# Slot pairs in four two-bank PSUM tiles, 1024-wide operations and one plan of step times, for a linear-attention and gMLP kernel

## Chip, cores, metric

One core of a Trainium2 chip. The time is the device time of one execution in microseconds (us). Five engines work side by side, each in the order of its own queue: TensorE (PE in the profile; its weight loads are PEld), VectorE (DVE), ScalarE (ACT), GpSimd (POOL) and SyncE (SP), which only issues DMAs here. PSUM is the memory that TensorE writes its results to; these kernels use it as eight banks, each for a tile of 128 x 512 fp32 values.

## The reference, cut to what matters

```python
# attention, for batch 8, heads 8, sequence 576, head width 64, 128 features
def phi(x):
    proj = x @ w_phi
    proj = proj - max(abs(proj), last axis)
    return concat([exp(proj), exp(-proj)])
q_p, k_p = phi(q), phi(k)
kv  = sum_s k_p v ;  z = sum_s k_p
x   = (q_p kv) / (q_p z + 1e-6)              # heads side by side: [8, 576, 512]
# gMLP block
h   = gelu_tanh(x @ w_in) ; u, v = halves of h
v_n = layernorm(v) * g_ln
v_s = w_sg @ v_n + b_sg                      # over the sequence
out = x + (u * v_s) @ w_out
```

## The kernel before: the parts that matter

The work is cut into eight halves k = 0 to 7 (two batches and four heads each) and four blocks u = 0 to 3 of gMLP. A half has nine slots of 128 rows. For each half: q and k are loaded (`qks`), merged into one tile (`qk`, VectorE), transposed (`qkT`, by DMA, for half 0 by TensorE), projected and exponentiated (`nat`, tiles `psk`, `psq`, `kp`), summed against the scaled values (`kvsum`, tile `pkv`; GpSimd scales the values), and turned into the attention output (`projnum`, tiles `pp`, `qp`, `pn`, `pxt`). Two halves feed one gMLP block: `win_v`, `norm`, `win_u`, `gate`, `wout`.

```python
psN = ctx.enter_context(tc.tile_pool(name="psN", bufs=4, space=PSUM))   # eight single banks
psA = ctx.enter_context(tc.tile_pool(name="psA", bufs=2, space=PSUM))   # in three pools
psM = ctx.enter_context(tc.tile_pool(name="psM", bufs=2, space=PSUM))

def load_qk(k, res, behind=None):
    qks = stage.tile([128, 2, HH, NS, D], FP16, tag="qks", name="qks")  # one buffer
    for t, src in enumerate((q, k_)):
        for ins in load(nc.gpsimd, ...):
            if behind is not None:                                      # held back behind the
                tc.add_manual_dep(ins.ins, behind.ins.name, sync, ...)  # transposes of a half
            yield
...
# nat, one slot: two banks, 512-wide operations
psk = psN.tile([128, HH, 128], F32, ...); psq = psN.tile([128, HH, 128], F32, ...)
... 4 + 4 matmuls ...
nc.vector.tensor_reduce(out=MK[:, n, :], in_=psk[:], axis=AX.X, op=ALU.max, ...)
nc.vector.tensor_reduce(out=MQ[:, n, :], in_=psq[:], axis=AX.X, op=ALU.max, ...)
for e in range(2):
    nc.scalar.activation(out=kp[:, e], in_=psk[:], func=AF.Exp, scale=(1.0, -1.0)[e])
...
# the main loop: the merge of half k+2 comes first, its load was issued during the stage before
qT[k + 2], last = prep(qks.pop(k + 2))
w.append((load_qk(k + 3, qks, last), 9, LD0, LD1))
weave(...)                       # interleaves the streams of one stage
...
# the last block
weave((win_v(res, range(NS)), 10, 0, 1))
weave((norm(res, 0, 5, (0, 1)), 7, 0, 0.5), (win_u(res, [(0, 288), (288, 288)]), 9, 0, 1))
weave((gate(res, 0), 9, 0, 1), (norm(res, 5, 9, ()), 6, 0, 0.5))
weave((win_u(res, [(576, 288), (864, 288)]), 9, 0, 1))
weave((wout(res, range(0, 4)), 5, 0, 1)); weave((gate(res, 1), 9, 0, 1)); weave((wout(res, range(4, 9)), 6, 0, 1))
```

## Time and profile before

| | before |
|---|---|
| time, median | 389.38 us (388.74 to 389.77, 3 runs) |
| span of the profiled execution | 381.7 us (this one execution took 383.46 us, a fast one) |
| busy: TensorE, VectorE, ScalarE, GpSimd | 291.3, 265.0, 246.3, 137.0 us |
| DMA: bytes moved, mean rate over the span | 40.04 MB, 105 GB/s |

The lines of the profile that matter are in the prediction. A row of the table of stretches is: start and end, length, then busy us and instruction count of PE, PEld, DVE, ACT, POOL, then the granted TensorE clock, the DMA share (mean busy share of 16 DMA engines; a little over 1 is possible as it is computed from packet times) and GB/s. A row of the timeline is: start, length, engine, line, operation, out<-in, shape, count, and in brackets how long the engine had been idle and what ended that. A row of the waits is: who waited <- for whom, then us in total, times, longest.

### The profile page before, as it was taken

How to read it: one execution, taken by the hardware profiler on the slowest of the kernel's cores; microseconds unless marked ns; L12 is line 12 of the kernel's file. 1: busy time of each engine (PE TensorE's matmuls, PEld its weight loads, DVE VectorE, ACT ScalarE, POOL GpSimd, SP SyncE). 2: the span in 40 equal slices, each digit the busy share in tenths (PEclk: the TensorE clock that was granted, in tenths of full speed). 3: DMA queues.
4: the chain of work that ended last, by engine and by line, in shares of the span. 5: the costliest groups of instructions: out<-in, count | busy, mean ns of one | idle time of the engine just before them, and what ended most of it. 6: DMA issues, size and time to landing. Idle time of an engine off the chain costs nothing.

```text
span 381.7 us, 7907 instructions
## 1 busy us (share of the span) xinstructions
PE 291.3 (76%) x3037; PEld 199.5 (52%) x3037; DVE 265.0 (69%) x680; ACT 246.3 (65%) x525; POOL 137.0 (36%) x173
## 2 busy tenths in 40 slices
PE   0263633847879989987896987977998898987894
PEld 0153522536645666754464765755566675644562
DVE  5499426876689998768569885675799944479230
ACT  1165314955986898569777892597779945672422
POOL 7247650592880229208800196046000830000000
PEclk9998585886589998999999899989999998799999
DMA  7996997288599705591992059902500020210024
GB/s 134 164 221 100 174 203 125 48 97 177 102 127 199 95 2 64 141 233 34 167 272 49 3 64 223 199 2 85 180 3 2 0 114 2 84 56 0 2 111 139
DMA packets 65094, 40.04 MB, mean 105 GB/s; under 512 B 36256, under 2 KB 61728, under 8 KB 65056
## 3 DMA queue, kind: packets, MB, share of 16 engines
q1 hardware_dynamic: 46128, 27.65, 29.3%
q0 software_dynamic: 18928, 11.88, 23.4%
q8 instruction: 24, 0.39, 0.4%
q14 instruction: 14, 0.11, 0.1%
HBM read 33.55 MB, written 9.44 MB: 113 GB/s over the span
## 4 chain that ended last, share of the span: by engine, by line
PE 29%; ACT 20%; DMA 14%; DVE 13%; POOL 12%; issue 9%; SPq 1%; ACTq 0%; DVEq 0%; POOLq 0%
DMA qks<-in_k_dram 8%; ACT qp L329 7%; ACT kp L258 7%; PE pu L399 5%; POOL qks L77 5%; POOL vx L274 5%; PE pw L439 4%; PE pv L383 4%; PE po L456 3%; PE pkv L313 2%; PE pn L348 2%; DVE bst L388 2%; DMA qkT<-qk 2%; DVE MK L252 2%; DMA wn<-in_moe_w_sg_dram 2%
## 5 line engine op out<-in xcount | busy, mean ns | idle before, releaser
L274 POOL TENSOR_TENSOR vx<-vs,vx 128x1024 f16<-128x1024 f32 (+2 forms) x48 | 72.1, 1520 | 104.0 <-ACT vx L265 100.0
L258 ACT ACTIVATE kp<-psk 128x512 f16<-128x512 f32 x144 | 81.7, 653 | 34.6 <-DVE MK L252 30.0
L329 ACT ACTIVATE qp<-pp 128x512 f16<-128x512 f32 x128 | 73.6, 685 | 15.8 <-PE pp L324 15.8
L252 DVE TENSOR_REDUCE MK<-psk 128x4 f32<-128x512 f32 x72 | 49.1, 681 | 8.6 <-PE psk L249 7.9
L254 DVE TENSOR_REDUCE MQ<-psq 128x4 f32<-128x512 f32 x72 | 49.0, 680 | 1.2 <-PE psq L251 1.2
L439 PE MATMUL pw<-WsgT,vt 128*128 128x288 f16 x256 | 45.8, 293 | 5.3 <-DVE uT L443 5.1
L249 PE MATMUL psk<-wk,qkT 128*128 128x128 f16 x288 | 33.8, 241 | 15.4 <-ACT qkT L232 9.6
L251 PE MATMUL psq<-wq,qkT 128*128 128x128 f16 x288 | 32.5, 242 | 15.2 <-DVE MQ L254 11.9
L443 DVE TENSOR_TENSOR uT<-pw,uT 128x288 f16<-128x288 f32 x64 | 28.6, 450 | 18.3 <-PE pw L441 16.5
L348 PEld LDWEIGHTS <-qp 128*128 128x128 f16 x512 | 23.8, 105 | 31.2 <-ACT qp L329 26.3
L348 PE MATMUL pn<-kvz,qp 128*128 128x65 f16 x512 | 29.5, 205 | 13.8 <-ACT qp L329 11.5
L401 ACT ACTIVATE uT<-pu 128x384 f16<-128x384 f32 (+1 forms) x52 | 24.3, 466 | 19.2 <-PE pu L399 18.4
L103 DVE COPY qk<-qks 128x2304 f16<-128x2304 f16 x16 | 14.6, 918 | 31.6 <-DMA qks<-in_k_dram 16.3
L460 ACT ACTIVATE osb<-po 128x512 f32<-128x512 f32 x36 | 24.2, 681 | 18.6 <-PE po L456 14.2
L399 PE MATMUL pu<-xT,Win 128*128 128x384 f16 (+1 forms) x208 | 35.6, 312 | 0.3 <-ACT vt L386 0.2
L383 PE MATMUL pv<-Win,xT 128*128 128x512 f16 x144 | 34.0, 384 | 1.2 <-ACT vt L386 1.1
L249 PEld LDWEIGHTS <-qkT 128*128 128x128 f16 x288 | 22.9, 108 | 22.6 <-ACT qkT L232 11.2
L439 PEld LDWEIGHTS <-vt 128*128 128x128 f16 x256 | 24.5, 99 | 18.6 <-issue 10.4
L251 PEld LDWEIGHTS <-qkT 128*128 128x128 f16 x288 | 23.5, 110 | 18.7 <-issue 17.4
L313 PE MATMUL pkv<-vx,kp 128*128 128x65 f16 x512 | 28.8, 208 | 5.0 <-POOL vx L274 5.0
L324 PE MATMUL pp<-qkT,wqm 66*128 66x512 f16 x72 | 29.8, 427 | 3.4 <-ACT kp L258 3.1
L456 PE MATMUL po<-Wout,uT 128*128 128x512 f16 x108 | 31.5, 386 | 0.0
(93 smaller groups left out, 520.6 us busy)
## 6 DMA issues: line engine op xcount, KB each, us to landing
out_dram<-osb SPq DMA_DIRECT2D x32, 256.0 KB
vs<-in_v_dram SPq DMA_DIRECT2D x16, 320.0 KB
vs<-in_v_dram SPq DMA_DIRECT2D x16, 256.0 KB
qks<-in_q_dram POOLq DMA_DIRECT2D x16, 160.0 KB, 4.0
qks<-in_k_dram POOLq DMA_DIRECT2D x16, 160.0 KB, 6.1
qks<-in_q_dram POOLq DMA_DIRECT2D x16, 128.0 KB, 4.7
qks<-in_k_dram POOLq DMA_DIRECT2D x16, 128.0 KB, 6.1
Win<-in_moe_w_in_dram POOLq DMA_DIRECT2D x1, 1024.0 KB, 10.8
```

The source lines that it names most:

```text
L249: nc.tensor.matmul(psk[:, i, :], qkT[:, n, i, :], wk[:], start=True, stop=True)
L251: nc.tensor.matmul(psq[:, i, :], qkT[:, n, i, :], wq[:], start=True, stop=True)
L252: nc.vector.tensor_reduce(out=MK[:, n, :], in_=psk[:], axis=AX.X, op=ALU.max, apply_absolute_value=True)
L254: nc.vector.tensor_reduce(out=MQ[:, n, :], in_=psq[:], axis=AX.X, op=ALU.max, apply_absolute_value=True)
L258: nc.scalar.activation(out=kp[:, e], in_=psk[:], func=AF.Exp, scale=(1.0, -1.0)[e])
L274: nc.gpsimd.tensor_tensor(out=vx[e][:, :, x0:x0 + nn, 0:64], in0=vs[:, :, n0:n1, :], in1=vx[e][:, :, x0:x0 + nn, 64:65].broadcast_to([128, ...
L329: nc.scalar.activation(out=qp[:, e], in_=pp[:], func=AF.Exp, scale=(1.0, -1.0)[e])
L348: nc.tensor.matmul(pn[:, i, :], lhs, rhs, start=(x == 0), stop=(x == len(terms) - 1))
L383: nc.tensor.matmul(pv[:], xT[:, c, n * 128:n * 128 + 128], Win[:, c, DF2:DFF], start=(c == 0), stop=(c == 3))
L399: nc.tensor.matmul(pu[:, 0:w], Win[:, c, d * 128:d * 128 + 128], xT[:, c, t0:t0 + w], start=(c == 0), stop=(c == 3))
L439: nc.tensor.matmul(pw[:], vts[5 * i + m][:, dd], WsgT[:, m, c0:c0 + 288], start=(m == 0), stop=False)
L456: nc.tensor.matmul(po[:], uT[:, d, cs], Wout[:, d, :], start=False, stop=(d == 3))
```

## The change

Its intent: fewer and wider instructions (slots 0-1, 2-3, 4, 5-6, 7-8 handled as groups), all PSUM in one pool of four two-bank tiles that every stage shares, loads ahead of time, and one list of step times for the whole kernel in place of stage-wise weaving. A step may demand that others have been emitted first. Cut to the core:

```diff
-    psN = ... bufs=4 ...   psA = ... bufs=2 ...   psM = ... bufs=2 ...
+    psX = ctx.enter_context(tc.tile_pool(name="psX", bufs=4, space=PSUM))
+    GROUPS = [(0, 1), (2, 3), (4,), (5, 6), (7, 8)]
+    def ps(name, dtype=F32):
+        return psX.tile([128, 2, 512 if dtype == F32 else 1024], dtype, tag="x", name=name)
...
-        qks = stage.tile([128, 2, HH, NS, D], FP16, tag="qks", name="qks")
+        qks = QKS[k] = stage.tile([128, 2, HH, NS, D], FP16, tag="qks", name="qks", bufs=2)
...   (no dependency of the loads on the transposes any more; three DMA transposes a half, not four)
-            nc.vector.tensor_reduce(out=MK[:, n, :], in_=psk[:], ...)          # 512 wide
+                reduce(MK[:, sl], kk)                                          # 1024 wide
...
-                nc.scalar.activation(out=kp[:, e], in_=psk[:], func=AF.Exp, ...)
+                nc.scalar.activation(out=kp[:, e]..., in_=kk[:, 0:ng], func=AF.Exp, ...)
...   (the same for qp, qmix, kvz, vt, uT, osb; rd, xs, xT, the gate products, the scaling by g)
+PLAN = {"turn0": (-2.48, -1.51), "nat0": (-1.91, -1.28), ..., "setup": (-0.12, 1), "w": 0.5, ...
+    "qk": (0.1, 0.38), "v": (0.65, 0.64), "nat": ..., "num": ...,
+    "gmlp": {"winv": ..., "winu": ..., "norm": ((0.5, 1.81),), "gate": ..., "wout": ...},
+    "last": {"winv": (0, 0.4), "winu": ((0.4, 0.8), (0.45, 1.71)), "norm": ((-0.39, 0.61), (1.21, 1)),
+             "gate": ((1.37, 1.9), (1.6, 2)), "wout": ((1.4, 1.6), (2, 2.4))}}
...
+    for _, _, stream in sorted(plan, key=lambda x: x[:2]):
+        stream.step()
```

## The prediction

> **What bounds the kernel now.** I read the page first (busy shares, the slices), then the table of stretches, then the waits and the timeline where the slices show a hole, and last the chain of work that ended last.
>
> The page: busy time of each engine, then three rows of the 40 slices.
>
> ```profile
> PE 291.3 (76%) x3037; PEld 199.5 (52%) x3037; DVE 265.0 (69%) x680; ACT 246.3 (65%) x525; POOL 137.0 (36%) x173
> ...
> PE   0263633847879989987896987977998898987894
> ...
> PEclk9998585886589998999999899989999998799999
> DMA  7996997288599705591992059902500020210024
> ```
>
> No engine is full, but TensorE is nearest to it, and its row falls into three parts: nine poor slices (to 86 us), then 7 to 9, then a tail. The same by stretches (busy us of each engine, with the instruction count; then granted clock, DMA share, GB/s):
>
> ```profile
> 0.00:30.00 30.00, 8.37 (x72) 7.05 (x73) 19.35 (x56) 10.21 (x20) 15.56 (x28) 1.00 1.03 174
> 30.00:62.00 32.00, 12.78 (x160) 11.03 (x158) 16.35 (x32) 8.87 (x21) 17.22 (x22) 0.69 0.84 148
> 62.00:100.00 38.00, 27.07 (x313) 19.56 (x313) 28.59 (x59) 28.91 (x67) 20.32 (x22) 0.72 0.73 126
> ...
> 140.00:180.00 40.00, 34.32 (x429) 24.33 (x426) 31.12 (x70) 31.11 (x74) 21.62 (x27) 0.96 0.53 113
> 180.00:220.00 40.00, 35.03 (x346) 22.49 (x344) 31.36 (x89) 31.36 (x64) 10.56 (x13) 0.96 0.60 117
> ...
> 340.00:381.70 41.70, 32.40 (x226) 19.99 (x223) 19.24 (x69) 13.54 (x29) 0.00 (x0) 0.98 0.16 58
> ```
>
> TensorE is idle 52 us of the first 100 (100 - 8.4 - 12.8 - 27.1), 29 us of the 240 in the middle (its seven middle stretches sum to 210.7 us busy) and 9 us of the last 42. In the middle, 80 us hold 69.4 us of TensorE and 62.5 us each of VectorE and ScalarE: TensorE leads, yet two others are at 78%, so any burst makes one wait for another. One round of two attention halves and one gMLP block takes 80 us: the chain shows the same piece at both ends of it.
>
> ```profile
> 167.35 1.57 ACT qp L329 x3
> ...
> 247.66 1.57 ACT qp L329 x3
> ```
>
> The hole in the slices at 51 to 63 us, in the timeline:
>
> ```profile
> 51.16 0.10 PEld L251 LDWEIGHTS <-qkT 128*128 128x128 f16 x1
> 58.05 0.76 DVE L103 COPY qk<-qks 128x2304 f16<-128x2304 f16 x1 [7.67 <-DMA qks<-in_q_dram]
> 61.02 0.76 DVE L103 COPY qk<-qks 128x2304 f16<-128x2304 f16 x1 [2.20 <-DMA qks<-in_k_dram]
> ...
> 61.81 0.69 DVE L252 TENSOR_REDUCE MK<-psk 128x4 f32<-128x512 f32 x1
> ...
> 63.15 0.59 PE L251 MATMUL psq<-wq,qkT 128*128 128x128 f16 x4 [11.77 <-DVE MQ L254]
> ```
>
> VectorE works in order. The merge of q and k for half 2 stands ahead of a reduction for half 1, and waits for a load that could be issued only when the one staging buffer was free and the transposes of half 1 were done. So every engine stops: 12 us without TensorE, after which its clock is low too. The waits give the sum of this kind over the kernel:
>
> ```profile
> ACT kp L258 <- DVE MK L252: 30.0, 14, 11.8
> ...
> DVE qk L103 <- DMA qks<-in_k_dram: 16.3, 6, 4.4
> ...
> DVE qk L103 <- DMA qks<-in_q_dram: 14.7, 3, 7.7
> ```
>
> Of the 31 us, 7 us are the first load, which stays; 24 us are later merges waiting for late loads.
>
> **What the Trainium skill says.** (1) "ScalarE: Activation LUTs", What ACT_TABLE_LOAD costs: an ACTIVATE with immediate operands takes 186 ns + 0.833 ns per element, and neighbours overlap by about 93 ns. The trace agrees roughly: 512 wide 653 ns (kp) and 597 ns (vt) against 613, 384 wide 491 against 506, and two exps back to back 0.98 us. (2) "VectorE: DVE Perf Modes", the section on the TRN2 errata: from PSUM, VectorE takes 120 + N cycles at 0.96 GHz, 658 ns for 512. The trace has 680, and starts of neighbouring reductions 0.60 us apart. (3) "Perfetto Trace Analysis", Optimizing Scalar/DVE Operations: larger operations help if the engine is saturated; if it is not but makes others wait, breaking instructions up may finish work sooner. Both halves bear on this change, in opposite directions. (4) "PSUM — Partial Sum Buffer", PSUM bank collisions: two engines must not use one bank at a time. The trace fits it: the exps of a key tile come only after its reduction.
>
> **The change part by part.**
>
> *Wider operations on ScalarE.* Five groups of slots (2, 2, 1, 2, 2) take the place of nine slots. Instructions: kp 144 to 80, qp 128 to 64, qmix 32 to 16, kvz 32 to 16, vt 36 to 20, uT 52 to 32, osb 36 to 20, qkT 9 to 5: 216 fewer, the same elements. What one saves: kp's busy time per instruction is 81.7/144 = 567 ns, of which 512 x 0.833 = 427 ns are elements, so 140 ns; in back-to-back pairs (0.98/2 = 490) only 63 ns. 216 x 63 to 140 ns = 14 to 30 us of 246; I take 22, or 5 us a round.
>
> *Wider operations on VectorE.* MK and MQ reductions 144 to 72, xs and rd 72 to 40 each, xT 24 to 16, gate products 64 to 32, scaling by g 32 to 16: 192 fewer. Each saves between 67 ns (0.60 us spacing less 533 ns of elements) and 147 ns (680 - 533): 13 to 28 us of 265; I take 20, or 5 us a round.
>
> *TensorE.* The same columns; win_u goes from 384-wide to 288-wide pieces, the gate takes each weight for two matmuls in a row but I assume that it is loaded twice. Busy time stays near 69 us a round; only in the first 100 us, where the clock was 0.7, can it fall.
>
> *Loads.* Two staging buffers for q and k, loads a whole round ahead of their merge, and each merge placed where its transposes are wanted. The 12 us hole at 51 us goes, unless the transfers themselves are too slow: the DMA share was 1.03 and 0.84 in the first two stretches, so only 0.16 x 32 = 5 us of engine time was free by 62 us. But weights for the gMLP (not needed before 100 us) are among it and now come behind q and k in the plan. Against that, values of half 0 are no longer held back behind the first merge, so the first load, which ended at 16 us, may end 2 to 3 us later. Net for the start: -12 + 3, and about -3 from a warmer clock and earlier transposes: -12 us. The later merges waited 2.3 to 4.4 us three times; TensorE was busy 7.98 of 8 and 8.72 of 9 us around two of these, so of their 9 us I count only 3.
>
> *Order in the middle.* From 109 to 130 us (win_v, norm, win_u) VectorE is busy 19.5 of 21 us and ScalarE 15.8: the norm is packed there. The plan spreads it over the next attention half. With 5 us less on two engines and this spread, I let a third of the 29 idle us of TensorE go: -10 us, the 3 us of late merges within it.
>
> *Tail.* Idle 9 us; TensorE stands 2.4 us on a gate product that queues behind the norm of the second half, and with two gMLP banks it fills one while the other is read. Four pairs and more win_u work beside the norm: -4 us.
>
> Sum: 389.4 - 12 - 10 - 4 = 363; I lean 2 us lower, since the wait chains from matmul to reduction to exp are passed half as often: 361 us.
>
> **The rivals.** (a) *PSUM becomes the bound.* Before there were eight single banks in three pools (4, 2, 2); now all stages share four pairs in turn. My estimate of one pair's life from the durations above: a key pair 0.5 (matmuls) + 1.2 (reduction) + 2 x 1.0 (exps) + waits = 4.2 us, query 3, pp 3, pn 2, output 3.4. With 74 tiles a round that is about 200 pair-us over 4 pairs, 50 us of a 75 us round: 67% full before any queueing, and TensorE, in order, stops at the first tile it cannot have. For it: ScalarE's queue lengthens each life. Against: no single stage is now confined to two banks. If true, the middle gains nothing or loses 5 to 10 us: 370 to 380. (b) *Coarse steps lengthen the chains*: a 1024-wide reduction, then two exps, before the first product; if TensorE has no other work between, waits on qp (26 us before weight loads) grow. 370 to 375. (c) *The start is transfer bound*: 12 us shrinks to 4: 369. (d) *All three parts pay in full* (VectorE and ScalarE at the high end, middle idle halved, start -18): 348.
>
> **Range and chances.** (a) and (c) together with half the tail gain give 378; (d) with a little more 346. Slower than 389 would need a badly ordered plan: PSUM pressure costing more than start and tail give. Faster by over 2% (under 381.6): 0.89; within 2%: 0.07; slower: 0.04.
>
> **What would show it.** ScalarE about 224 us and VectorE 245 us busy, 1024-wide exps near 1.0 us and reductions near 1.2 us: the arithmetic of widths. No wait of a merge on a load after the first two, TensorE at work at 51 to 63 us: the loads. TensorE idle under 40 us in its first 100 us. A round near 76 us. Wrong would be: rows in which matmuls wait for ScalarE or VectorE to free a PSUM pair, growing to tens of us; VectorE still waiting for loads at 40 to 60 us; merges far above 0.76 us in their new layout; more table loads than eight.

## The result and the profile after

| | before | after |
|---|---|---|
| time, median | 389.57 us (388.74 to 393.25, 4 runs) | 366.88 us (365.67 to 367.83, 4 runs) |
| ratio | | 0.9399 (95% interval 0.9333 to 0.9464) |
| span of the profiled execution | 381.7 us | 365.1 us |
| instructions of ScalarE, VectorE | 525, 680 | 309, 488 |

A ratio here is the mean time of one kernel's fast runs over that of the other's in the same rounds, so it is not quite the ratio of the medians. The chips of the different experiments differ by about 1% for the kernel before, so I compare kernels by their ratios to it.

Busy time and the slices of the changed kernel:

```profile
PE 276.4 (76%) x3085; PEld 201.2 (55%) x3085; DVE 251.3 (69%) x488; ACT 228.4 (63%) x309; POOL 136.9 (38%) x173
...
PE   0082505747579998698899958888999869999994
...
DMA  7994999989919900988269000770530011021034
```

The reader sees ScalarE and VectorE 17.9 and 13.7 us lower. But the first ten slices of TensorE are as poor as before, and the DMA row under them is nearly all 9. So I cut both traces where every run can be aligned: ScalarE loads its gelu table once per block, just before the first gelu. The five stretches (start; three rounds; tail) of the kernel before, then of the changed one:

```profile
0.00:110.89 110.89, 57.24 (x640) 44.32 (x640) 72.54 (x165) 57.97 (x131) 62.58 (x88) 0.78 0.82 139
110.89:185.53 74.64, 65.89 (x754) 44.68 (x753) 61.80 (x157) 59.73 (x129) 32.40 (x40) 0.98 0.61 112
185.53:267.52 81.99, 69.42 (x754) 47.53 (x751) 60.59 (x152) 60.71 (x129) 30.88 (x35) 0.94 0.59 119
267.52:333.82 66.30, 61.03 (x651) 40.61 (x650) 46.90 (x128) 49.63 (x104) 11.19 (x12) 0.95 0.17 55
333.82:381.70 47.88, 37.72 (x249) 22.34 (x247) 23.20 (x78) 18.29 (x35) 0.00 (x0) 0.98 0.17 61
```

```profile
0.00:110.53 110.53, 49.96 (x614) 41.85 (x614) 70.16 (x123) 54.21 (x78) 66.69 (x95) 0.76 0.94 156
110.53:186.89 76.36, 68.61 (x788) 48.53 (x789) 58.16 (x108) 55.80 (x77) 36.33 (x43) 0.96 0.67 121
186.89:260.42 73.53, 64.11 (x754) 46.73 (x752) 58.05 (x102) 56.09 (x77) 22.77 (x24) 0.95 0.39 94
260.42:322.41 61.99, 56.13 (x661) 40.00 (x660) 42.18 (x89) 45.66 (x60) 11.13 (x12) 0.97 0.16 52
322.41:365.10 42.69, 37.58 (x272) 24.07 (x270) 22.73 (x68) 16.68 (x20) 0.00 (x0) 0.97 0.22 81
```

Length against length: the start gained 0.4 us (110.9 to 110.5), the first two rounds 6.7 (156.6 to 149.9), the third 4.3, the tail 5.2: together the 16.6 us between the two spans. The rest of the 22.7 us between the medians is that the profiled execution of before was a fast one (383.46 us, its timed runs are near 389). How that slack is spread over its stages no trace here shows, so each gain of a stage against the kernel before could be up to 6 us larger than these rows say. The two kernels also do their steps in a different order, so a stage of one is not exactly the work of that of the other.

The hole that the prediction wanted closed is closed, and another stands in its place, in the timeline of the changed kernel:

```profile
57.67 1.71 DVE L194 COPY b<-wn 128x640 f16<-128x640 f16 x4 [9.68 <-DMA wn<-in_moe_w_sg_dram]
...
58.22 0.71 PE L201 MATMUL pst<-ident,b 128*128 128x128 f16 x5 [12.17 <-DVE b L194]
...
59.83 1.94 ACT L367 ACTIVATE qp<-pp 128x1024 f16<-128x1024 f32 x2 [10.99 <-PE pp L354]
```

TensorE stands for 12 us because the first transposes of the set-up (spatial weights `w_sg`) are queued ahead of the first projections `pp`. They wait for a load `wn` that now comes behind q and k of halves 2 and 3: its DMAs were issued at 34.8 to 49.5 us, before at 6.7 to 22.6 us. Before, q and k waited and `wn` was early; now it is the other way round.

A second new hole, 6 us of TensorE at 78 to 84 us:

```profile
76.22 6.56 DVE L114 COPY qk<-qks 128x2304 f16<-128x2304 f16 x1
...
76.34 1.50 POOL L296 TENSOR_TENSOR vx<-vs,vx 128x768 f16<-128x768 f32 x1
...
78.65 3.52 POOL L296 TENSOR_TENSOR vx<-vs,vx 128x768 f16<-128x768 f32 x3
...
84.27 1.04 PE L386 MATMUL pn<-kvz,qp 128*128 128x65 f16 x16 [6.06 <-DVE xs L390]
```

A merge copy that takes 0.75 us when alone took 6.56 us, from the start of a chain of GpSimd's scalings to its end, and the division that TensorE needed stood behind it. The Trainium skill, page "SBUF — State Buffer", section Who interferes with whom, says that VectorE copies in a two-port mode and GpSimd share a port pair, and that whoever issues first makes the other block fully. The trace fits it: a GpSimd instruction begun at 75.76 us was under way when the copy started, the last of the chain ended at 82.17 us and the copy 0.6 us later. In which mode the copy ran no trace shows. In the kernel before the longest merge was 1.9 us; over the kernel the merges cost 21 us of VectorE in place of 15.

### The profile page after: what moved, and what is told of

The parts are those of the page before. It is cut to its first block, busy times and chain, and to the rows that moved or that the text cites. A ratio compares the mean times of both kernels' runs of the same rounds, so it can differ in the third digit from the quotient of the medians.

```text
span 365.1 us, 7547 instructions
## 1 busy us (share of the span) xinstructions
PE 276.4 (76%) x3085; PEld 201.2 (55%) x3085; DVE 251.3 (69%) x488; ACT 228.4 (63%) x309; POOL 136.9 (38%) x173
## 4 chain that ended last, share of the span: by engine, by line
PE 38%; ACT 23%; DVE 18%; DMA 9%; issue 5%; POOL 4%; SPq 1%; DVEq 0%; POOLq 0%; ACTq 0%
ACT kp L278 9%; PE pv L425 9%; ACT qp L367 8%; PE po L521 6%; PE pw L505 5%; DMA qks<-in_k_dram 4%; PE pn L386 3%; DVE MX L259 3%; POOL vx L296 2%; DVE vt L475 2%; DMA wn<-in_moe_w_sg_dram 2%; PE pu L448 2%; DVE vt L482 2%; PE pkv L340 2%; DVE qk L114 2%
## 5 line engine op out<-in xcount | busy, mean ns | idle before, releaser
L278 ACT ACTIVATE kp<-kk 128x1024 f16<-128x1024 f32 (+1 forms) x80 | 70.9, 950 | 12.3 <-DVE MX L259 12.2
L367 ACT ACTIVATE qp<-pp 128x1024 f16<-128x1024 f32 x64 | 62.8, 1037 | 15.7 <-PE pp L354 15.7
L259 DVE TENSOR_REDUCE MX<-kk 128x8 f32<-128x1024 f32 x40 | 48.5, 1215 | 19.8 <-PE kk L256 19.6
L259 DVE TENSOR_REDUCE MX<-qq 128x8 f32<-128x1024 f32 x32 | 38.8, 1214 | 0.7 <-PE qq L256 0.7
L448 PE MATMUL pu<-xT,Win 128*128 128x288 f16 x256 | 32.5, 286 | 0.0
L507 DVE TENSOR_TENSOR uT<-pw,uT 128x576 f16<-128x576 f32 x32 | 23.8, 752 | 12.6 <-PE pw L505 12.2
L256 PE MATMUL kk<-wk,qkT 128*128 128x128 f16 x288 | 25.5, 236 | 8.2 <-DVE xs L390 2.9
L431 DVE BATCH_NORM_STATS2 bst<-vt 128x6 f32<-128x512 f16 x36 | 23.7, 678 | 11.3 <-ACT vt L428 11.2
L448 PEld LDWEIGHTS <-Win 128*128 128x128 f16 x256 | 24.6, 98 | 6.2
L450 ACT ACTIVATE uT<-pu 128x576 f16<-128x576 f32 x32 | 20.8, 650 | 10.5 <-PE pu L448 10.5
L428 ACT ACTIVATE vt<-pv 128x1024 f16<-128x1024 f32 (+1 forms) x20 | 18.2, 937 | 13.7 <-PE pv L425 13.7
```

The source lines that it names most:

```text
L256: nc.tensor.matmul(out[:, 128 * i:128 * i + 128], qkT[:, n, i, :], w[:], start=True, stop=True)
L259: nc.vector.tensor_reduce(out=out, in_=in_.rearrange("p s (h x) -> p s h x", h=HH), axis=AX.X, op=ALU.max, apply_absolute_value=True)
L278: nc.scalar.activation(out=kp[:, e].rearrange("p s h x -> p s (h x)"), in_=kk[:, 0:ng], func=AF.Exp, scale=(1.0, -1.0)[e])
L367: nc.scalar.activation(out=qp[:, e].rearrange("p s h x -> p s (h x)"), in_=pp[:], func=AF.Exp, scale=(1.0, -1.0)[e])
L448: nc.tensor.matmul(pu[:, s, 0:288], Win[:, c, d * 128:d * 128 + 128], xT[:, c, t0:t0 + 288], start=(c == 0), stop=(c == 3))
L507: nc.vector.tensor_tensor(out=us, in0=pw[:, :, 0:288], in1=us, op=ALU.mult)
```

## The experiments

All twelve kernels gave correct results. The table first, so that each run can be placed; "first gelu" is the first gelu table load in the run's trace, "two rounds" from it to the third such load, "rest" from there to the end of the span.

| run | median us | ratio to before (95%) | first gelu | two rounds | rest |
|---|---|---|---|---|---|
| before (profiled) | 389.57 | 1 | 110.9 | 156.6 | 114.2 |
| changed | 366.88 | 0.940 (0.933 to 0.946) | 110.5 | 149.9 | 104.7 |
| e1 set-up late | 364.51 | 0.943 (0.937 to 0.949) | 108.6 | 150.9 | 104.6 |
| e2 narrow | 378.82 | 0.980 (0.974 to 0.986) | 114.8 | 156.9 | 105.8 |
| e3 three pairs | 398.08 | 1.033 (1.026 to 1.039) | 120.6 | 166.7 | 109.1 |
| e4 before + loads | 371.23 | 0.961 (0.957 to 0.966) | 106.2 | 150.9 | 112.5 |
| e5 half 1 by TensorE | 366.77 | 0.942 (0.935 to 0.948) | 111.0 | 149.5 | 105.1 |
| e6 halves 1, 2 | 357.38 | 0.917 (0.911 to 0.924) | 102.0 | 148.6 | 105.0 |
| e7 halves 1, 2, 3 | 357.72 | 0.918 (0.912 to 0.925) | 101.3 | 148.8 | 104.7 |
| e8 old tail order | 370.12 | 0.951 (0.943 to 0.959) | 110.8 | 148.4 | 108.4 |
| e9 e5 + two merged | 368.89 | 0.944 (0.938 to 0.951) | 114.8 | 147.0 | 105.1 |
| e10 e4 + tail order | 366.34 | 0.940 (0.933 to 0.947) | 105.3 | 151.2 | 109.1 |
| e11 e6 + two merged + values held | 357.21 | 0.918 (0.911 to 0.924) | 104.8 | 148.3 | 105.1 |
| e12 e10 + halves 1, 2 | 358.25 | 0.924 (0.914 to 0.933) | 98.6 | 148.2 | 109.1 |

My first theory: the start lost its gain to queue order alone (the set-up ahead of the projections). The rival: the transfers bind the first 100 us, so that each hole closed opens another. For the rest: width pays, or the plan and the loads do.

**e1, the set-up a stage later.**

```diff
-    "kv0": (-0.91, -0.35), "setup": (-0.12, 1), "w": 0.5, ...
+    "kv0": (-0.91, -0.35), "setup": (1.0, 2.0), "w": 0.5, ...
```

> The changed kernel with one number of its plan changed: the set-up of the spatial weights (its load, its VectorE copies, its five TensorE transposes) moved from just before the first output half to a whole stage later. Theory (head of line): TensorE stood 12.2 us at 46 to 58 us because the set-up's transposes were queued ahead of the first projections and waited for a load that now comes behind two more halves of q and k; the 12 us hole of before was moved, not removed. Then the hole goes and the time falls by 8 to 13 us, to 354 to 359. Rival (transfers bind the start): something else waits for its load in the same stretch, the first gelu still starts near 110 us, and the time changes by less than 3 us.

Measured: ratio 0.943, no better than the changed kernel's 0.940; the first gelu 2 us earlier. The hole at 46 us went, and this came (timeline of e1):

```profile
73.11 3.94 DVE L114 COPY qk<-qks 128x2304 f16<-128x2304 f16 x1 [7.50 <-DMA qks<-in_k_dram]
...
77.80 1.04 PE L386 MATMUL pn<-kvz,qp 128*128 128x65 f16 x16 [11.06 <-DVE xs L390]
```

The merge of half 3 now waits for its load, then for GpSimd; TensorE stands 11 us for it. My theory of what the hole cost fell; the rival stood: the wait moved to the next transfer.

**e2, narrow operations in the same pairs and plan.** Each of the 1024-wide exps, the gelus, output copies, reductions, divisions, gate products and the scaling by g was cut in two:

```diff
-                nc.scalar.activation(out=kp[:, e]..., in_=kk[:, 0:ng], func=AF.Exp, ...)
+                for s_ in range(ng):
+                    nc.scalar.activation(out=kp[:, e, s_]..., in_=kk[:, s_], func=AF.Exp, ...)
-                reduce(MK[:, sl], kk)
+                for s_, n in enumerate(g):
+                    reduce(MK[:, n:n + 1], kk[:, s_:s_ + 1])
```

> The changed kernel with the same pair tiles, the same plan, but every 1024-wide operation of ScalarE (exps, gelus, output copies) and VectorE (reductions, divisions, gate products, scaling by g) cut back into two of half the width. Theory (width pays in the middle): ScalarE's and VectorE's busy time go back up by about 18 and 18 us, and the time rises by 8 to 16 us (375 to 383), most of it after the first gelu at 110 us. Rival (the plan and the loads did it, width is hidden): the time rises by less than 3 us.

Measured: ratio 0.980 against 0.940, some 12 us more by the medians (on different chips) and 16 by the ratios, as the theory had it; by the profiled executions 4 us in the start, 7 in the two rounds, 1 in the rest. ScalarE's busy time rose by 11.8 us (228.4 to 240.2) for 192 more instructions, 61 ns each. VectorE's rose by 5.7 us (251.3 to 257.0), but its merges were 7 us shorter in this run, so 12.7 us for 176 instructions, 72 ns each. The groups of e2 and of the changed kernel (busy us and mean ns of one):

```profile
L371 ACT ACTIVATE qp<-pp 128x512 f16<-128x512 f32 x128 | 68.0, 648 | 20.9 <-PE pp L357 20.9
```

```profile
L367 ACT ACTIVATE qp<-pp 128x1024 f16<-128x1024 f32 x64 | 62.8, 1037 | 15.7 <-PE pp L354 15.7
```

One wide exp reads 1037 ns and two narrow ones 1296, which looks like 259 ns saved; but the busy times differ by 5.2 us for 64 instructions fewer, 81 ns each. Neighbouring instructions overlap, and the mean duration counts the overlap twice.

**e3, three pairs.** `psX` with `bufs=3`.

> The changed kernel with three PSUM pairs in place of four. If PSUM is near its limit (my rival a: 67 per cent full by estimate), losing a quarter makes TensorE wait for pairs everywhere: plus 20 us or more. If four pairs have slack, it costs less than 8 us.

Measured: ratio 1.033, 36 us more than the changed kernel by the ratios and 31 by the medians. The waits of TensorE at 100 to 340 us have rows that the changed kernel has not:

```profile
PE pw L505 <- DVE MX L259: 5.8, 3, 1.9
PE pw L505 <- ACT qp L367: 5.3, 5, 1.2
```

A gate product `pw` needs no reduction and no exp; it waits for the PSUM pair that these were reading. In the changed kernel `pw` waits for neither. So my rival (a) was near: a fourth pair cannot be spared.

**e4, the kernel before with the loads of the change.**

```diff
-        qks = stage.tile([128, 2, HH, NS, D], FP16, tag="qks", name="qks")
+        qks = stage.tile([128, 2, HH, NS, D], FP16, tag="qks", name="qks", bufs=2)
         for _ in load_qk(1, qks): pass
+        for _ in load_qk(2, qks): pass
...
-                    w.append((load_qk(k + 3, qks, last), 9, LD0, LD1))
+                    w.append((load_qk(k + 3, qks), 9, LD0, LD1))
```

> The kernel before with one part of the change alone: two staging buffers for q and k, and loads not held behind the transposes. Theory: its 12 us hole at 51 to 63 us (the merge of half 2 waiting for its load) shrinks to under 4 us and the time falls by 8 to 12 us, to 377 to 381, since its set-up comes before the loads of half 2. Rival (transfers bind the start, whoever comes first): the hole moves to another wait and the time falls by less than 4 us.

Measured: ratio 0.961, more than I gave it: 5.7 of the changed kernel's 6.7 us in the two rounds (156.6 to 150.9), and 4.7 us in the start (both against the fast profiled execution of before). The hole of 51 to 63 us is gone, and again a part of it comes back later, now at a third place, the one merged buffer that the DMA transposes of half 2 still read (timeline of e4):

```profile
74.18 0.76 DVE L103 COPY qk<-qks 128x2304 f16<-128x2304 f16 x1 [10.31 <-DMA qkT<-qk]
```

**e5, e6, e7: transposes of more halves by TensorE**, on top of e1. These take 36 TensorE instructions and five ScalarE copies a half, and take 1.2 MB of transposes from the DMA engines.

```diff
-        at(("turn", k), turn_t, 6 if first else 2, lambda k=k: turn_pe(k) if k == 0 else turn(k),
+        at(("turn", k), turn_t, 6 if k in (0, 1, 2) else 2, lambda k=k: turn_pe(k) if k in (0, 1, 2) else turn(k),
```

> The late set-up of the run before, and the transposes of half 1 done by TensorE and ScalarE (as those of half 0 are) in place of three DMA transposes. Theory (the DMA engines bind the first 100 us, so each hole that is closed opens another): taking 1.2 MB of transposes off them lets the first gelu start 3 to 6 us earlier, and the time falls to 358 to 362. Rival (order of the engines' queues binds, not the DMA): less than 1.5 us against 364.5.

> The same with halves 1 and 2 transposed by TensorE. Theory (DMA bound start): another 3 to 5 us, 354 to 359. Rival: no further gain, or a loss, as ten more PSUM pairs and 5 us of ScalarE copies fall into the busy first stage.

> The same with halves 1, 2 and 3 transposed by TensorE. By then the first stages should no longer be bound by the DMA engines: I expect within 2 us of the run with halves 1 and 2, either way.

Measured: half 1 alone gained nothing (0.942; a miss of my expectation). Halves 1 and 2 gave 0.917, the first gelu 8.5 us earlier than in the changed kernel; half 3 nothing more. The trace of e5 shows why one half was not enough (VectorE's timeline, then SyncE's queue, whose row covers the issuing of five transposes, waits included):

```profile
73.48 0.76 DVE L114 COPY qk<-qks 128x2304 f16<-128x2304 f16 x1 [18.86 <-DMA qkT<-qk]
```

```profile
41.48 39.85 SPq L123 DMA_TRANSPOSE qkT<-qk x5
```

The three transposes of half 2 were issued one after another at 41.5, 47.9 and 56.0 us, and landed at 57, 65 and 73 us by the semaphores in the trace: 16 to 17 us each. Over the whole changed kernel the median of a DMA transpose from issue to landing is 5.0 us. The Trainium skill, page "Trainium Kernel Development and Optimization", section Key Constraints, says that DMAs from all queues run on the same 16 DMA engines and interleave. In e5 these were at a share of 1.14 at 30 to 62 us. That fits a small transfer, needed next, that waits among megabytes needed later; no run shows it for a transpose alone.

**e9, a second merged buffer on top of e5**, to tell the held buffer from the late transposes:

```diff
-        qk = QK[k] = stage.tile([128, NS, HH, 2, D], FP16, tag="qk", name="qk")
+        qk = QK[k] = stage.tile([128, NS, HH, 2, D], FP16, tag="qk", name="qk", bufs=2)
```

> The run with half 1 transposed by TensorE (366.8 us), with two merged q-and-k buffers in place of one (and two buffers in place of three for the divided numerators, to make room). There VectorE waited 18.9 us at 54 to 73 us to write the merge of half 3, until the DMA transposes of half 2, which crawl while the DMA engines are saturated, had read the one merged buffer. Theory (it is the held buffer that stops the engines, the slow transfers alone do not): that wait goes, the first gelu comes 6 to 12 us earlier, and the time falls to 355 to 361. Rival (the transfers bind by themselves: half 2 is needed next and is not there): the first gelu stays within 3 us of 111 us and the time within 363 to 368.

Measured: ratio 0.944, nothing gained; the first gelu at 114.8 us and the time at 368.9, both a little beyond the rival's range. The theory's gain did not come, but the test is not clean: the order of the queues changed, one buffer for `xs` was given up, and VectorE waited at other places, the last of them for the merge of half 4, whose buffer the transposes of half 2 still held (timeline of e9). So a held buffer is not ruled out as part of the cause.

```profile
77.57 0.76 DVE L114 COPY qk<-qks 128x2304 f16<-128x2304 f16 x1 [12.16 <-DMA qkT<-qk]
```

**e8, the old order in the last block of the changed kernel**: the second half of `win_u` after the first gate.

```diff
-        "winv": (0, 0.4), "winu": ((0.4, 0.8), (0.45, 1.71)), "norm": ((-0.39, 0.61), (1.21, 1)),
-        "gate": ((1.37, 1.9), (1.6, 2)), ...
+        "winv": (0, 0.4), "winu": ((0.4, 0.8), (1.2, 1.4)), "norm": ((0.4, 0.6), (0.81, 1)),
+        "gate": ((0.8, 1.2), (1.6, 2)), ...
```

> The changed kernel with the last block in the order of the kernel before: the second half of win_u after the first gate, not beside the norm. Theory (order made the tail's 5 us): the tail from the last gelu table load grows from 42.7 to 46 to 48 us and the time rises by 3 to 5 us, to 370 to 372. Rival (the four pairs made it, in place of two banks): the tail stays within 1.5 us.

Measured: ratio 0.951, 3.2 us more by the medians (on different chips; 4.3 by the ratios, whose intervals overlap), as the theory said. But the increase is not where I put it: the tail grew only by 1.1 us (43.8), the third round by 2.7, since in the changed kernel output steps of the block before also lie in the tail (272 TensorE instructions there, here 249). The "rest" of the table, which holds both, is the fair measure: 104.7 against 108.4. TensorE's timeline, e8 first, then the changed kernel:

```profile
330.78 4.08 PE L448 MATMUL pu<-xT,Win 128*128 128x288 f16 x32
336.88 3.50 PE L505 MATMUL pw<-WsgT,vt 128*128 128x288 f16 x14 [2.02 <-DVE vt L482]
```

```profile
332.06 8.00 PE L448 MATMUL pu<-xT,Win 128*128 128x288 f16 x64
339.90 1.15 PE L505 MATMUL pw<-WsgT,vt 128*128 128x288 f16 x8
```

With 64 matmuls of `win_u` ahead of the gate the norm is done when the gate starts; with 32 TensorE waits for it.

**e10, the kernel before with the loads of e4 and the new order of the last block**; single banks, three pools, narrow operations.

```diff
-                weave((norm(res, 0, 5, (0, 1)), 7, 0, 0.5), (win_u(res, [(0, 288), (288, 288)]), 9, 0, 1))
-                weave((gate(res, 0), 9, 0, 1), (norm(res, 5, 9, ()), 6, 0, 0.5))
-                weave((win_u(res, [(576, 288), (864, 288)]), 9, 0, 1))
+                weave((norm(res, 0, 5, (0, 1)), 7, 0, 0.4), (norm(res, 5, 9, ()), 6, 0.4, 0.8),
+                      (win_u(res, [(0, 288), (288, 288), (576, 288), (864, 288)]), 17, 0, 1))
+                weave((gate(res, 0), 9, 0, 1))
```

> The kernel before with its early loads (371.2 us) and the changed order of the last block: all of win_u beside the two norms, ahead of the gates; narrow operations, eight single banks in three pools as before. If pairs and wide operations are worth little by themselves, this comes within 3 us of the changed kernel: 366 to 370, with a tail of 43 to 45 us. If the tail's gain needed the four shared pairs, the tail stays at 47 to 48 us and the time at 370 to 372.

Measured: ratio 0.940, the same as the changed kernel within 0.7%, with a tail of 44.5 us against 48.0 in e4. So two small edits of the old kernel give the whole gain, and the tail's part needs no pairs. The stretches show that the pair layout with its plan is not without effect: after the first gelu the changed kernel is 5.7 us shorter (254.6 against 260.3), and up to it 5.2 us longer (110.5 against 105.3). The two cancel.

**e11, e6 with two merged buffers and the first values held behind the first merge** (as the kernel before held them).

> The best so far (set-up late, halves 1 and 2 transposed by TensorE, 357.4 us) with two merged buffers and the values of half 0 held behind the first merge, as the kernel before did. Theory: the first transposes start 2 to 3 us earlier only if the first merge was slowed by the values; 353 to 357. Rival: the values then come too late for the first scaling, and nothing is gained: 357 to 360.

Measured: 0.918, as e6. The first gelu even came later (104.8 against 102.0). Inconclusive on each of its two edits by itself; together they bring nothing.

**e12, the kernel before with loads, order of the last block, and halves 1 and 2 by TensorE.**

```diff
-        qT[1], last = prep(qks.pop(1))
+        _, qT[1], slot1 = turn_qk(qks.pop(1))
+        for n in range(NS):
+            slot1(n)
...
+                if k == 0:
+                    _, qT[2], slot2 = turn_qk(qks.pop(2))
+                    w.append(((slot2(n) for n in range(NS)), 10, 0, 0.9))
```

> The kernel before with its early loads and the changed tail (ratio 0.940 to before), and halves 1 and 2 transposed by TensorE and ScalarE: no pairs, no wide operations, three PSUM pools. Theory (the transfers bind the first 100 us in either kernel, and the pair layout nets nothing): the same step as in the changed kernel, ratio 0.915 to 0.925, the first gelu at 96 to 101 us. Rival (it was the plan of the changed kernel that could use the freed DMA engines, or two single gMLP banks choke on the extra transposes): 0.935 or more.

Measured: ratio 0.924, the first gelu at 98.6 us, 6.7 us earlier than in e10. So the step belongs to the start, not to the layout. It ties with e6 within the intervals. Both beat the kernel before and the changed one: e6 (357.38 us) is the changed kernel with the two lines of e1 and e6 altered.

## Why the prediction was right

The time was inside the range (346 to 378), 5.9 us above the 361 predicted, and the gain 22.7 us in place of 28.4. The sum is better than its terms, and that is partly luck: the largest term, the start, failed as far as the profiles show, and 6 of the 22.7 us lie in no stage that they locate. Loads and the order of the tail give the whole gain in the old kernel (e10), so pairs, width and plan together brought nothing more. Two slips of its working: the middle has six stretches, not seven (the sum is right), and the upper end of 378 does not follow from its terms (start -4, middle 0, tail -2 and the 2 us of the lean give 381). Step by step:

**Start, -12 us: wrong.** It measured -0.4 us between the profiled executions. Of the signs, TensorE was to be idle under 40 us of its first 100; it was idle 57 us (before: 52), and one merge took 6.6 us, a named sign of being wrong. The step that failed is "weights for the gMLP (not needed before 100 us) ... now come behind q and k in the plan": not needed for the result, but the set-up's transposes of one of those weights stood in TensorE's queue ahead of half 0's projections, so they were needed at 46 us. And my rival (c), the start bound by transfers, was more than the correction of 8 us that I gave it. The DMA share of the start rose from 0.82 to 0.94, closing the new hole gained 2 us of the start and nothing in the ratio (e1), and what did shorten the start of the changed kernel was to take transposes off the DMA engines (e6; e12 in the old one). The merge beside GpSimd held TensorE a further 6 us once.

**Late merges, 3 us within the middle: too small.** The loads alone gave the old kernel 5.7 us over two rounds (e4): TensorE's busy time there stayed (135.3 and 135.5 us) and its idle time fell from 21.3 to 15.5 us. I take it that ScalarE and GpSimd come late behind a waiting VectorE, and TensorE, busy at that moment, stands afterwards; no run isolates that path. I had looked only at TensorE's busy share in the stretch of the wait.

**Middle, -10 us: the size right (-11.0 over three rounds), the reason only in part.** Loads alone gave the old kernel 5.7 us in the first two rounds, where the whole change gave 6.7. Width was worth 12 to 16 us in the pair layout (e2), but the pair layout and its plan with narrow operations are themselves worse than the old kernel with early loads and the new tail (0.980 against 0.940), so what width gives pays back what pairs and plan take. Pairs and plan were never tried apart.

**Width, 63 to 147 ns an instruction: the lower end.** 61 ns on ScalarE and 72 ns on VectorE (e2, busy time), so by estimate 216 x 61 ns = 13 us where I took 22, and 192 x 72 ns = 14 us where I took 20. I had the low figures in hand, from back-to-back pairs, and took the middle.

**Tail, -4 us: right in size, and in one of its two reasons.** -5.2 us; the order of `win_u` is worth about 3 to 4 us of the time (e8). The four pairs, named as well, are not needed for it: single banks got 3.4 us of the rest by the order alone (e10 against e4).

**Rival (a), PSUM as the bound: right in kind.** A fourth of the PSUM less costs 31 to 36 us (e3), so the estimate of 67% full before queueing was a fair warning. With four pairs the rows in which `kk`, `qq` and `pp` wait for `kp`, `MX` or `xs`, which I read as waits for a pair, sum to 12 us at 100 to 340 us; the like rows of the kernel before (`psk`, `psq`, `pp` after `kp` or `MQ`) sum to 10. That is not the tens of us that were named as the sign of being wrong.

What stays open: whether it is the bytes or the way in which DMA transposes share the engines that binds the first 100 us; no run measured a transpose by itself, and e9 did not part them from the held buffer. And where the pair layout loses up to 5 us before the first gelu is only bounded (set-up order, merges against GpSimd), not split.

## What to carry to other kernels

When a stall on a transfer is removed by loading earlier, ask which transfer is now later and which in-order queue has something behind it; here, with the DMA engines at a share near 1 over the first 100 us, moving the wait about gained nothing more and fewer transfers did. Price a wider instruction by the difference of busy times in back-to-back runs, not by the durations of single ones, and count what the wider tile does to the number of buffers. And before a rewrite, try its two or three separable parts in the old kernel: here an additional staging buffer with early loads and one moved stage of the last block gave the same time as the new layout.

## What the Trainium skill lacked or had wrong

- "ScalarE: Activation LUTs", What ACT_TABLE_LOAD costs: 186 ns + 0.833 N less an overlap of about 93 ns leaves, by that sum, about 93 ns for each ACTIVATE saved; cutting wide activations in two cost 61 ns each here (11.8 us of busy time for 192). The section does not say whether its tile lay in SBUF or PSUM; all 192 here read PSUM, so this is a gap, not shown to be an error.
- "SBUF — State Buffer", Who interferes with whom: says that the other side blocks for the whole instruction; here one VectorE copy of 0.75 us was held through a whole chain of GpSimd instructions, 6.56 us (and in e1 through another, 3.94 us). That a chain can hold it is not said.
- "Perfetto Trace Analysis", Matmul Optimizations, asks that all eight PSUM banks be used; both kernels do. It has no figure for how few tiles are too few: four two-bank tiles against three was 366.9 against 398.1 us here (ratios 0.940 and 1.033).
- No page that I read says how slow a DMA transpose becomes on busy DMA engines: 5.0 us median over the changed kernel; in e5, at a DMA share of 1.14, 16 to 17 us each, and 32 us for three in a row.
